# Mask rows moved in four pieces instead of eight, and three steps of an attention schedule moved, in an attention and mixture-of-experts kernel

## The chip, the cores and the metric

The kernel runs on one core of one Trainium2 chip. The metric is the device time of one execution in microseconds (us), as the median of several runs. PE is the matrix engine (TensorE) and PEld its weight loads, DVE is VectorE, ACT is ScalarE, POOL is GpSimd, and SP is the engine whose queue issues most of the DMAs.

## The reference

Three layers follow one another. The first is an attention in which a query sees only keys that fall to the same of 16 centroids:

```
q_assign = np.argmax(np.einsum('bhsd,hcd->bhsc', q_n, c_n), axis=-1)
k_assign = np.argmax(np.einsum('bhsd,hcd->bhsc', k_n, c_n), axis=-1)
mask = q_assign[:, :, :, None] == k_assign[:, :, None, :]
scores = scale * np.matmul(q, k.transpose(0, 1, 3, 2))
scores = np.where(mask, scores, -1000000000.0)
attn = softmax(scores)
return np.matmul(attn, v)
```

There are 2 batches of 8 heads, 768 positions and 64 dimensions a head. The second layer sends each of the 1536 tokens to one of 8 experts (512 to 1024 to 512), the third is a gated unit (512 to 1536 to 512). Only the first layer's code is changed.

## The kernel before, in words

The attention works on pairs of heads, eight of them (n = 0 to 7), and each pair has 12 steps: 2 heads times 6 blocks of 128 queries, so 96 steps g in all. In every step the function `run` walks through a fixed list of tokens, `CFG["order"]`, and each token issues some instructions. Since every engine works through its own instructions in order, this list sets the order on each engine. `S` is `soft(g + 1)`: ACT computes the exponential `P` of a block's scores, with the row maximum as bias. `Q` is `qk(g + 2)`: PE computes the scores `s` of a block two steps ahead (four matmuls, `Ak`/`Aq` and then `kB`/`qB`), and DVE takes their negative row maximum `nm`. `T0` and `T1` are `pt(g, 0)` and `pt(g, 1)`: PE transposes `P` in two halves of three blocks into `t`, and ACT copies the first half to `PT`, DVE the second. `E` is `evac`: in the second of every three steps it takes the output sum `acc` out of PSUM, half of it through ACT (`ol`), and DVE adds the two halves into `O`. `O` is `onat`: where `outs` has an entry, PE brings the output into natural order (`on`) and DVE computes the reciprocal sums `rs` and writes logits `lg` and outputs `x`. `V0` is `pv`: in the first of every three steps PE multiplies `PT` with v into `acc`. `B0` and `B1` issue the preparation of the next pair.

The preparation has eight parts, each at a step that `CFG["offs"]` gives relative to the first step of the pair that is running. `q0`, `q1`, `k0`, `k1` (function `tr`) transpose half of the next pair's q or k (`trp`); ACT and DVE or POOL split them into a high part `H`, a low part `L` and a sum `X`, and after the second half SP issues the moves of `H` and `L` into the tiles `A` and `B` that the scores read. `a` (`assign`) multiplies `X` with the centroids (`asp`, copied by ACT to `as`). `t` (`pick`) transposes that (`ast`), and DVE takes the maximum and marks where it is met (`mxa`, `eqa`). `f` makes the one-hot rows `oh`, and `m` (`mask`) transposes them (`otp`), ACT writes them, scaled for k to 0 and a large negative number, to `oT`, and SP moves 16 rows each into `qB` and `kB`. The scores of a block come out masked that way, by 16 more rows of the contraction.

The PSUM tile that `trp`, `asp`, `ast`, `otp` and `on` write, tag `mm` of pool `ps_m`, exists once. The scores have two buffers (`ps_s`), the transposes of `P` two (`ps_t`), `acc` one (`ps_a`). For a half of a pair whose index is not the last, `outs` puts `on` at step 0 (half 0) or 3 (half 1) of the following pair, as `CFG["oc"]` says; in the last pair other numbers hold.

Of the kernel before, what the change touches and what calls it, by code (L numbers as in the profile page):

```python
# [11 lines left out]
F32R = mybir.dt.float32r  # L12
I32 = mybir.dt.int32
U32 = mybir.dt.uint32
AF = mybir.ActivationFunctionType
# [8 lines left out]
class Attention:  # L24
# [119 lines left out]
    def tr(self, n, nm, half):  # L144
# [10 lines left out]
        nc.scalar.activation(out=Ht[:, sl], in_=flat, func=AF.Copy, scale=s)  # L155
        if CFG["xe"]["qk".index(nm)] == "a":
            nc.scalar.activation(out=X[:, sl], in_=flat, func=AF.Copy, scale=s)
# [130 lines left out]
    def mask(self, n):  # L288
        nc, st = self.nc, self.pairs[n]
        C, HJ, HS = self.C, self.J // 2, self.S // 2  # L290
        oT = self.one.tile([128, HS], F32R, tag="oT", name="oT")
        ps = self.ps_m.tile([128, HJ, 128], F32, tag="mm", name="otp")
        for jj in range(HJ):
            nc.tensor.transpose(ps[:, jj, :], st["oh"][:, jj, :], self.ident)
        nc.scalar.activation(out=oT, in_=ps.rearrange("p j t -> p (j t)"), func=AF.Identity, scale=self.sc[:, 0:1],
                             bias=self.sc[:, 1:2])
        for half in range(2):
            sl = slice(half * HS, (half + 1) * HS)
            for si, nm in enumerate("qk"):
                Bt = st["B" + nm]  # L300
                r0 = (2 * half + si) * 2 * C
                self.move(Bt[64:64 + C, 0, sl], oT[r0:r0 + C])
                self.move(Bt[64 - C:64, 1, sl], oT[r0 + C:r0 + 2 * C])

    def prep_steps(self, n):
        return dict(q0=lambda: self.tr(n, "q", 0), k0=lambda: self.tr(n, "k", 0), q1=lambda: self.tr(n, "q", 1),
# [122 lines left out]
    def run(self, cent, gate, early, fill, after):  # L429
# [6 lines left out]
        for n in range(1, self.NP):  # L436
            s0 = 2 * J * (n - 1)
            st = self.prep_steps(n)
            for nm, o in CFG["offs" if n > 1 else "offs1"]:
                if n == 1 and nm in ("q0", "q1"):  # L440
                    continue
                bg.setdefault(s0 + o, []).append(st[nm])
            if n + 1 < self.NP:
                bg.setdefault(s0 + CFG["load"], []).append(lambda n=n: self.load(n + 1, "qk"))
            if n > 1:
# [31 lines left out]
        for G in range(4 * self.NP - 1):  # L477
            n, half, r = self.group(G)
            if r == 1:
                outs[(G + 1) * HJ + CFG["oc"][half if n + 1 < self.NP else 2]] = n, half  # L480

        def trickle(g, tok):
            if chains and tok in CFG["mt" if g < NG - 2 * J else "mt2"] and g >= chains[0][0]:
                if next(chains[0][1]) is None:
                    moves.append(chains.pop(0)[1])
            if moves and tok == CFG["pt"] and g % CFG["pe"] == 0:
                if next(moves[0], 0) == 0:
                    moves.pop(0)
# [44 lines left out]
            pass  # L533


CFG = {'px': 'a', 'mt2': ['T0', 'S'], 'mt': ['B1'], 'pt': 'V0', 'pe': 1, 'ms': [5, 2, 1], 'mr': 5, 'order': ['S', 'Q', 'T0', 'T1', 'E', 'B0', 'O', 'V0', 'B1'], 'offs': [['q0', -4], ['q1', -2], ['k0', -1], ['k1', 1], ['a', 2], ['t', 3], ['f', 6], ['m', 7]], 'xe': 'da', 'me': 'a', 'ee': 'a', 'ec': 1, 'oc': [3, 3, 2], 'offs1': [['q0', 4], ['k0', 0], ['k1', 1], ['a', 2], ['t', 3], ['f', 5], ['m', 6], ['q1', 0]], 'load': 0}


class Router:
# [662 lines left out]
```

## Time and profile before

| | |
|---|---|
| median of 3 runs | 826.34 us (826.06 to 828.03) |
| the profiled execution | 829.75 us, of which the trace's span is 827.7 us |
| PE busy in the span | 785.4 us (95%) |
| DVE, ACT, POOL busy | 531.2, 380.8, 191.9 us |
| granted clock of PE, mean | 0.993 of full speed |

The profile is of one execution. The attention lasts from the start to about 300 us, the experts to about 525, the gated unit to the end. Busy time of PE is no measure of its speed, since matmuls are pipelined and their ends are modelled; where PE is held up is read from the waits and from the distances of starts.

### The profile page before, as it was taken

To read this page: it belongs to the slowest core of one execution; us is meant where nothing else is said; L and a number is where in the kernel's file an instruction comes from. 1 tells how busy PE (TensorE), PEld (TensorE's weight loads), DVE (VectorE), ACT (ScalarE), POOL (GpSimd) and SP (SyncE) were. 2 spreads that over 40 slices of the span, in tenths; PEclk is the share of its full clock that TensorE was granted. 3 is DMA by queue.
4 is the path that set the end of the run, shared out by engine and by line. 5 is a ranking of instruction groups with operands and counts; after the bars stand their busy time and mean duration, and the time that the engine had idled before them with its cause. 6 is when DMAs were issued, how large, how long until landed. Compare 5 with 4: busy or idle time off the path is not lost. (4 is left out here: it accounts for less than half of the span.)

```text
span 827.7 us, 12686 instructions
## 1 busy us (share of the span) xinstructions
PE 785.4 (95%) x4791; PEld 656.6 (79%) x4791; DVE 531.2 (64%) x871; ACT 380.8 (46%) x697; POOL 191.9 (23%) x212
## 2 busy tenths in 40 slices
PE   7998999988989998999999999999999999999996
PEld 6766666656756678999999997878888888888885
DVE  5675676766776775765665563677767676667433
ACT  5674675755666644455454452444423223222110
POOL 5110110101120145500000000244333323332335
PEclk9999999999999999999999999999999999999999
DMA  9864848527153127666665751223221212210012
GB/s 201 191 135 131 209 129 246 128 63 173 28 155 111 39 92 265 216 212 195 195 204 192 227 170 50 85 93 103 76 77 56 72 51 76 72 57 1 0 52 101
DMA packets 94209, 102.03 MB, mean 123 GB/s; under 512 B 30752, under 2 KB 78752, under 8 KB 94144
## 3 DMA queue, kind: packets, MB, share of 16 engines
q1 hardware_dynamic: 89280, 89.33, 38.2%
q0 software_dynamic: 1920, 6.29, 2.0%
q10 hardware_dynamic: 2944, 5.54, 1.9%
q8 instruction: 41, 0.67, 0.4%
q14 instruction: 24, 0.20, 0.1%
HBM read 68.21 MB, written 12.58 MB: 98 GB/s over the span
## 5 line engine op out<-in xcount | busy, mean ns | idle before, releaser
L341 DVE TENSOR_REDUCE nm<-s 128x1 f32<-128x768 f32 x96 | 91.4, 953 | 71.3 <-PE s L338 70.7
L351 ACT ACTIVATE P<-s,nm 128x768 f32<-128x768 f32 x96 | 87.0, 907 | 9.4 <-DVE nm L341 5.8
L370 ACT COPY PT<-t 128x384 f32<-128x384 f32 x96 | 46.3, 482 | 84.9 <-PE t L367 84.3
L367 PE MATMUL t<-ident,P 128*128 128x128 f32 x576 | 82.1, 277 | 0.9 <-ACT PT L370 0.5
L1027 POOL TENSOR_TENSOR W1l<-cm,W1h 128x512 fp32r<-128x512 f32 x18 | 23.4, 1303 | 235.0 <-ACT W1h L1026 235.0
L367 PEld LDWEIGHTS t<-ident,P 128*128 128x128 f32 x576 | 69.7, 143 | 7.4 <-DVE PT L372 1.2
L844 PE MATMUL hp<-Xl,W1h 128*128 128x256 f32 x256 | 73.3, 286 | 0.3 <-DVE Xl L837 0.3
L844 PE MATMUL hp<-Xh,W1h 128*128 128x256 f32 x256 | 73.3, 286 | 0.2 <-ACT Xh L836 0.2
L844 PE MATMUL hp<-Xh,W1l 128*128 128x256 f32 x256 | 73.1, 285 | 0.0
L844 PE MATMUL yp<-Hhh,W2h 128*128 128x256 f32 x256 | 73.1, 285 | 0.0
L844 PE MATMUL yp<-Hhh,W2l 128*128 128x256 f32 x256 | 72.5, 283 | 0.0
L844 PE MATMUL yp<-Hhl,W2h 128*128 128x256 f32 x256 | 72.4, 283 | 0.0
L386 PE MATMUL acc<-PT,ldv 128*64 128x384 f32 x384 | 69.7, 495 | 0.2 <-DVE rm L634 0.2
L1054 POOL TENSOR_TENSOR ghl<-u,ghh 128x512 fp32r<-128x512 f32 x36 | 49.9, 1385 | 75.0 <-ACT ghh L1053 75.0
L338 PE MATMUL s<-Ak,Aq 128*128 128x384 f32 x192 | 59.1, 389 | 6.6 <-ACT P L351 6.6
L1073 DVE TENSOR_TENSOR acc<-o,acc 128x512 f32<-128x512 f32 x60 | 41.2, 692 | 31.0 <-PE o L1065 31.0
L1051 DVE TENSOR_TENSOR u<-sg,g 128x512 f32<-128x512 f32 x36 | 24.8, 688 | 54.0 <-ACT sg L1050 54.0
L338 PE MATMUL s<-kB,qB 80*128 80x384 f32 (+1 forms) x192 | 52.1, 347 | 5.6 <-DMA kB<-oT 4.8
L338 PEld LDWEIGHTS s<-Ak,Aq 128*128 128x128 f32 x192 | 29.3, 192 | 32.8 <-ACT P L351 23.1
L1053 ACT CAST ghh<-u 128x512 fp32r<-128x512 f32 x36 | 22.4, 622 | 67.9 <-DVE u L1052 67.9
L372 DVE COPY PT<-t 128x384 f32<-128x384 f32 x96 | 52.5, 547 | 1.3 <-PE t L367 1.3
L844 PEld LDWEIGHTS hp<-Xl,W1h 128*128 128x128 f32 x256 | 49.9, 195 | 0.5 <-DVE Xl L837 0.5
(269 smaller groups left out, 1972.7 us busy)
## 6 DMA issues: line engine op xcount, KB each, us to landing
raw<-in_moe_w SPq DMA_DIRECT2D x64, 512.0 KB, 4.3
Ak<-Hk SPq DMA_DIRECT2D x32, 192.0 KB, 4.8
moe_rows<-zero SPq DMA_DIRECT2D x8, 768.0 KB, 5.6
raw<-in_moe_w_gate SPq DMA_DIRECT2D x12, 512.0 KB, 3.6
raw<-in_moe_w_val SPq DMA_DIRECT2D x12, 512.0 KB, 3.6
raw<-in_moe_w_out SPq DMA_DIRECT2D x12, 512.0 KB, 3.5
xr<-moe_rows ACTq DMA_DIRECT2D x7, 768.0 KB, 6.2
ldq<-in_q SPq DMA_DIRECT2D x16, 192.0 KB, 4.2
```

Source lines behind the costliest of these rows:

```text
L338: nc.tensor.matmul(ps[:, c, 0:HS], lhsT=ql[:, qs], rhs=kr[:, c * HS:(c + 1) * HS], start=a == 0, stop=a == 1)
L341: nc.vector.tensor_reduce(out=nm, in_=ps[:, :, 0:HS], axis=AX.XY, op=ALU.max, negate=True)
L351: nc.scalar.activation(out=P, in_=ps[:, :, 0:HS], func=AF.Exp, bias=nm, accum_out=self.pairs[n]["sum"][:, i, r:r + 1])
L367: nc.tensor.transpose(ps[:, jj, :], P[:, a, jj * 128:(jj + 1) * 128], self.ident)
L370: nc.scalar.copy(out=PT[:, js, cs], in_=ps)
L372: nc.vector.tensor_copy(PT[:, js, cs], ps)
L386: nc.tensor.matmul(acc[c * D:(c + 1) * D], lhsT=v[:, c * HJ + j], rhs=PT[:, c * HJ + j, :], start=j == 0, stop=j == HJ - 1, tile_position= ...
L844: self.nc.tensor.matmul(out, lhsT=W[a][:, k, cols], rhs=mov[b][:, k, :], start=i == 0, stop=i == n - 1)
L1027: nc.gpsimd.tensor_tensor(out=l, in0=m, in1=h.bitcast(F32), op=ALU.subtract)
L1051: nc.vector.tensor_tensor(out=u, in0=sg, in1=ps[0], op=ALU.mult)
L1054: nc.gpsimd.tensor_tensor(out=hl[:, fc], in0=u, in1=hh[:, fc].bitcast(F32), op=ALU.subtract)
L1073: nc.vector.tensor_tensor(out=a, in0=p[t], in1=a, op=ALU.add)
```

## The change

Three things are changed. The mask rows: `mask` writes the two halves of the sequence side by side into an `oT` of 64 rows and 768 columns, by two ACT instructions of 64 partitions each, and moves 16 rows of 768 columns by four DMAs, where there was one ACT instruction of 128 partitions and eight DMAs of 16 rows and 384 columns. The order of tokens: `E` stands behind `S`, in front of `Q`, and no longer behind `T1`. The steps: `q1` runs at -3 in place of -2, and the natural-order output of half 1 at 4 in place of 3.

```
     def mask(self, n):
         nc, st = self.nc, self.pairs[n]
         C, HJ, HS = self.C, self.J // 2, self.S // 2
-        oT = self.one.tile([128, HS], F32R, tag="oT", name="oT")
+        oT = self.one.tile([4 * C, 2 * HS], F32R, tag="oT", name="oT")
         ps = self.ps_m.tile([128, HJ, 128], F32, tag="mm", name="otp")
         for jj in range(HJ):
             nc.tensor.transpose(ps[:, jj, :], st["oh"][:, jj, :], self.ident)
-        nc.scalar.activation(out=oT, in_=ps.rearrange("p j t -> p (j t)"), func=AF.Identity, scale=self.sc[:, 0:1],
-                             bias=self.sc[:, 1:2])
         for half in range(2):
-            sl = slice(half * HS, (half + 1) * HS)
-            for si, nm in enumerate("qk"):
-                Bt = st["B" + nm]
-                r0 = (2 * half + si) * 2 * C
-                self.move(Bt[64:64 + C, 0, sl], oT[r0:r0 + C])
-                self.move(Bt[64 - C:64, 1, sl], oT[r0 + C:r0 + 2 * C])
+            p = slice(half * 4 * C, (half + 1) * 4 * C)
+            nc.scalar.activation(out=oT[:, half * HS:(half + 1) * HS], in_=ps[p].rearrange("p j t -> p (j t)"),
+                                 func=AF.Identity, scale=self.sc[p, 0:1], bias=self.sc[p, 1:2])
+        for si, nm in enumerate("qk"):
+            for r, p0 in ((0, 64), (1, 64 - C)):
+                c0 = (2 * si + r) * C
+                self.move(st["B" + nm][p0:p0 + C, r], oT[c0:c0 + C])
...
-CFG = {'px': 'a', 'mt2': ['T0', 'S'], 'mt': ['B1'], 'pt': 'V0', 'pe': 1, 'ms': [5, 2, 1], 'mr': 5, 'order': ['S', 'Q', 'T0', 'T1', 'E', 'B0', 'O', 'V0', 'B1'], 'offs': [['q0', -4], ['q1', -2], ['k0', -1], ['k1', 1], ['a', 2], ['t', 3], ['f', 6], ['m', 7]], 'xe': 'da', 'me': 'a', 'ee': 'a', 'ec': 1, 'oc': [3, 3, 2], 'offs1': [['q0', 4], ['k0', 0], ['k1', 1], ['a', 2], ['t', 3], ['f', 5], ['m', 6], ['q1', 0]], 'load': 0}
+CFG = {'px': 'a', 'mt2': ['T0', 'S'], 'mt': ['B1'], 'pt': 'V0', 'pe': 1, 'ms': [5, 2, 1], 'mr': 5, 'order': ['S', 'E', 'Q', 'T0', 'T1', 'B0', 'O', 'V0', 'B1'], 'offs': [['q0', -4], ['q1', -3], ['k0', -1], ['k1', 1], ['a', 2], ['t', 3], ['f', 6], ['m', 7]], 'xe': 'da', 'me': 'a', 'ee': 'a', 'ec': 1, 'oc': [3, 4, 2], 'offs1': [['q0', 4], ['k0', 0], ['k1', 1], ['a', 2], ['t', 3], ['f', 5], ['m', 6], ['q1', 0]], 'load': 0}
```

The changed file is one line shorter from `mask` on, so a line of `qk` that is L338 before is L337 after.

On PE, steps 3 and 4 of a middle pair. Before:

```order
L338 MATMUL s<-kB_93,qB_91 128x384 x2
L367 MATMUL t<-ident,P 128x128 x6
L213 MATMUL ast<-ident,as 128x128 x3
L416 MATMUL on<-R,O 128x144 x3
L386 MATMUL acc<-PT,ldv 64x384 x6
L338 MATMUL s<-Ak,Aq 128x384 x2
L338 MATMUL s<-kB_93,qB_91 128x384 x2
L367 MATMUL t<-ident,P 128x128 x6
```

And in the changed kernel, on the same engine at the same place:

```order
L337 MATMUL s<-kB_93,qB_91 128x384 x2
L366 MATMUL t<-ident,P 128x128 x6
L213 MATMUL ast<-ident,as 128x128 x3
L385 MATMUL acc<-PT,ldv 64x384 x6
L337 MATMUL s<-Ak,Aq 128x384 x2
L337 MATMUL s<-kB_93,qB_91 128x384 x2
L366 MATMUL t<-ident,P 128x128 x6
L415 MATMUL on<-R,O 128x144 x3
```

The output matmuls `on` have moved from behind `ast` to behind the next step's transposes of `P`.

On ACT, steps 7 to 10 of a middle pair. Before:

```order
L351 ACTIVATE P,sum<-s,nm 128x768
L370 COPY PT<-t 128x3x128
L397 COPY ol<-acc 64x384
L295 ACTIVATE oT<-otp,sc 128x384
L351 ACTIVATE P,sum<-s,nm 128x768
L370 COPY PT<-t 128x3x128
L155 ACTIVATE Hq<-trp 128x384
L351 ACTIVATE P,sum<-s,nm 128x768
L370 COPY PT<-t 128x3x128
L351 ACTIVATE P,sum<-s,nm 128x768
L370 COPY PT<-t 128x3x128
L397 COPY ol<-acc 64x384
```

And in the changed kernel, from the same exponential on:

```order
L350 ACTIVATE P,sum<-s,nm 128x768
L396 COPY ol<-acc 64x384
L369 COPY PT<-t 128x3x128
L297 ACTIVATE oT<-otp,sc 64x384 x2
L350 ACTIVATE P,sum<-s,nm 128x768
L369 COPY PT<-t 128x3x128
L155 ACTIVATE Hq<-trp 128x384
L350 ACTIVATE P,sum<-s,nm 128x768
L369 COPY PT<-t 128x3x128
L155 ACTIVATE Hq<-trp 128x384
L350 ACTIVATE P,sum<-s,nm 128x768
L396 COPY ol<-acc 64x384
```

The evacuation `ol` has moved in front of the copy of `PT`, `oT` is two instructions, and the second `Hq` follows the first after one exponential.

On SP's queue, from the first mask move of a middle pair to q's first moves. Before:

```order
L132 DMA qB_90<-oT 16x384 x2
L132 DMA kB_92<-oT 16x384 x2
L132 DMA qB_90<-oT 16x384 x2
L132 DMA kB_92<-oT 16x384 x2
L132 DMA Aq<-Hq 64x768
L132 DMA qB_91<-Hq 64x768
```

And in the changed kernel, on the same queue:

```order
L132 DMA qB_90<-oT 16x768 x2
L132 DMA kB_92<-oT 16x768 x2
L132 DMA Aq<-Hq 64x768
L132 DMA qB_91<-Hq 64x768
L132 DMA Aq<-Lq 64x768
```

The first mask move into `kB` is the third in the queue; before, the first one for half 1 was the seventh.

## Rows read from the trace of the kernel before

**Rows 1.** Waits of PE, 36 to 322 us: engine, line, releaser: us, times, longest.

```profile
PE on L416 <- DVE rs L411: 10.1, 6, 1.7
PE s L338 <- ACT P L351: 4.9, 14, 0.9
PE s L338 <- DMA kB<-oT: 4.8, 6, 1.8
...
PE trp L151 <- DVE Lq L160: 1.7, 5, 0.3
```

**Rows 2.** Waits of the weight loads in the same stretch.

```profile
PEld on L416 <- issue: 11.3, 6, 1.9
...
PEld asp L203 <- issue: 1.2, 6, 0.2
```

**Rows 3.** Timeline of PE, 93 to 146: start, us, operation, count, [idle before, releaser].

```profile
98.05 0.97 PE L416 MATMUL on<-R,O 128*128 128x144 f32 x6 [1.68 <-DVE rs L411]
...
101.85 0.82 PE L367 MATMUL t<-ident,P 128*128 128x128 f32 x6
102.42 0.59 PE L338 MATMUL s<-Ak,Aq 128*128 128x384 f32 x2
...
103.21 0.94 PE L367 MATMUL t<-ident,P 128*128 128x128 f32 x6
104.43 0.61 PE L338 MATMUL s<-Ak,Aq 128*128 128x384 f32 x2 [0.28 <-ACT P L351]
...
109.54 0.49 PE L294 MATMUL otp<-ident,oh 128*128 128x128 f32 x3
...
116.81 0.44 PE L338 MATMUL s<-kB,qB 80*128 80x384 f32 x1 [0.35 <-DMA kB<-oT]
...
119.95 0.55 PE L151 MATMUL trp<-ident,ldk 128*128 128x128 f32 x3 [0.34 <-DVE Lq L160]
```

**Rows 4.** Timeline of DVE in the same stretch.

```profile
102.12 0.96 DVE L341 TENSOR_REDUCE nm<-s 128x1 f32<-128x768 f32 x1 [2.39 <-PE s L338]
...
122.57 0.17 DVE L411 TENSOR_SCALAR rs<-sum 128x6 f32<-128x6 f32 x1
...
123.19 0.55 DVE L420 TENSOR_TENSOR x<-on,rs 128x384 f32<-128x384 f32 x1
```

**Rows 5.** Groups of instructions, 40 to 430 us: count, busy us, mean ns, idle before.

```profile
L370 ACT COPY PT<-t 128x384 f32<-128x384 f32 x89 | 42.9, 482 | 81.7 <-PE t L367 81.0
...
L399 DVE TENSOR_TENSOR O<-acc,ol 64x384 f32<-64x384 f32 x31 | 16.9, 546 | 0.6
...
L397 ACT COPY ol<-acc 64x384 f32<-64x384 f32 x31 | 14.8, 476 | 2.7 <-PE acc L386 1.9
```

**Rows 6.** Timeline of ACT, 93 to 146 us.

```profile
102.88 0.48 ACT L397 COPY ol<-acc 64x384 f32<-64x384 f32 x1
103.38 0.90 ACT L351 ACTIVATE P<-s,nm 128x768 f32<-128x768 f32 x1
...
110.42 0.67 ACT L295 ACTIVATE oT<-otp,sc 128x384 fp32r<-128x384 f32 x1
110.99 0.89 ACT L351 ACTIVATE P<-s,nm 128x768 f32<-128x768 f32 x1
```

**Rows 7.** SP's timeline, then the list of DMAs: count, KB each, us to landing.

```profile
114.92 1.22 SPq L132 DMA_DIRECT2D kB<-oT  x2
...
kB<-oT SPq DMA_DIRECT2D x28, 24.0 KB, 1.9
...
qB<-oT SPq DMA_DIRECT2D x1, 48.0 KB, 2.9
kB<-oT SPq DMA_DIRECT2D x1, 48.0 KB, 2.5
```

**Rows 8.** Stages: us, busy (count) of PE, PEld, DVE, ACT, POOL, PEclk, DMA, GB/s.

```profile
189.00:191.20 2.20, 2.20 (x12) 2.10 (x11) 1.97 (x5) 1.36 (x3) 1.00 (x1) 0.50 0.46 102
...
358.00:411.00 53.00, 52.70 (x440) 52.35 (x440) 33.01 (x35) 27.05 (x35) 0.00 (x0) 1.00 0.66 208
```

## The prediction

> **What bounds the kernel now.** I read four views: the waits of TensorE (PE), its timeline through one pair of heads, ACT and DVE beside it, and the stages. In the expert part PE is busy 52.70 of 53 us while the DMA engines move at 0.66 [rows 8], so nothing but less PE work helps there; the change doesn't touch it. In the attention PE stands still some five us in every pair, and the waits view says for what: the output matmul `on` behind DVE's `rs` (10.1 us, six times), scores behind ACT's exponential (4.9), scores behind the mask moves (4.8, six times, longest 1.8), transposes of k behind `Lq` (1.7, five times) [rows 1]. The reader should see that three of these four come in the same number as the middle pairs: they are stalls of the schedule's pattern, not accidents. They also cost more than they show: PE's ends are modelled, so an idle of 0.28 before the scores at 104.43 goes with a start-to-start distance of 1.22 us after the transposes at 103.21, where the same six transposes at 101.85 give way after 0.57 [rows 3]. 0.65 was lost, 0.28 is shown. I add 0.25 to an idle, less than that difference, where no such pair of rows stands. PE's weight loads say the same of `on`: 11.3 us over six, 1.9 each, against 1.68 of idle [rows 2, 3].
>
> I count the twelve steps of a pair from 0; qk runs two steps ahead, so step 10 issues the next pair's first scores.
>
> **`on`, one step later (half 1: `oc` 3 to 4).** At step 3 `pick` puts its transposes `ast` into the only buffer of `ps_m`, and `on` wants the same buffer at once. It waits until DVE has taken the maximum and `eqa` out: 1.9 us. At step 4 the buffer has long been read, since the 2 us of `acc` and a whole step lie between. The 1.9 goes, six times. The 0.65 lost at 104.43 goes too: between the scores of steps 4 and 6 PE now has `on` as well (0.97 us busy [rows 3]), and that is longer than the wait for P. What is late next: DVE's four instructions of the outputs take 1.17 us from the first to the last when nothing holds them (122.57 to 123.74) [rows 4] and fall into two short steps without `acc`, so the second half of step 6's transposes waits for step 5's PT copy on DVE. That costs between 0 and 1.17; by DVE's sequence from 102.12 on (maximum, copy, these four, maximum, copy: about 5.1 us after the scores start, where PE wants its buffer at 4.7) I take 0.35. Moving `on` between transposes and scores loses some 0.2 in changes of kind (estimate from the distances above). Per pair 1.9 + 0.65 - 0.35 - 0.2 = 2.0; **six pairs, 12.0 us**.
>
> **Mask moves, four for eight.** The moves run in one queue, SP, 1.22 us for two; in the old order the one that the first scores need is the seventh, issued at 114.92, and PE goes on at 116.81, 1.89 later [rows 3, 7]. Now it is the third, so 1.25 after the first, with 48 KB in place of 24. The median landing of 24 KB is 1.9; the two 48 KB moves of the first pair took 2.9 and 2.5 [rows 7]. The price: ACT now evacuates 64 partitions twice, and a copy of 64 partitions (476 ns) is no cheaper than one of 128 (482) [rows 5]. One oT blocks ACT 0.57 us, from 110.42 to the P at 110.99 [rows 6]. otp ends at 110.03 [rows 3], so two of them put that P at about 111.25, 0.25 later, and PE waits for this P (one of the 14 waits in [rows 1]): 0.25 is on the path. The second oT ends near 111.35, the third move starts at 112.6 and lands by 115.1 to 115.5; PE asked at 116.81 - 0.35 = 116.46, so it no longer waits: 0.35 + 0.25 = 0.6 gone.
> The Trainium skill, page "DMA: Bandwidth & Descriptors", section "Anatomy of one DMA", gives a DMA a fixed cost of about 2.0 us that doesn't grow with size; by it (an estimate) the 48 KB would land in about 2.1. The 24 KB rows agree and the 48 KB rows don't (2.5 and 2.9), perhaps for what else was then in flight. By the rule the sum is the same, since nobody waits either way; the second rival below would have 0.04 in place of 0.08.
>
> **q1 one step earlier (-2 to -3).** Its three transposes are moved, not added. k's transposes at step 11 waited 0.34 for `Lq` of q1 [rows 1, 3], 0.6 with the hidden part; now two steps lie between. q1 itself follows q0 by one step, as k0 followed q1, but no O stands before `Lq` there any more, and the longer wait for P gives it time: taken as 0. Its six DMAs leave one step sooner behind only four mask moves on SP; they wait for q's own halves there, so no load is held up. Without O's distance, step 11's second transposes may wait for a PT copy: 0 to 0.55 (one O, 546 ns [rows 5]), I take 0.3. With the masks: 0.6 + 0.6 - 0.25 - 0.3 = 0.65; **five pairs, 3.2 us**.
>
> **The late ones.** Of the six waits for moves four are near 0.35, so 4.8 - 6 x 0.35 = 2.7 lies in two late landings. Behind one of them the granted clock is 0.50 for 2.2 us [rows 8], the lower of the two levels: 1.1 us of work. With a margin of 1 us or more most of both should be gone: **3.8 us**, but irregular; an execution without late landings has none of it to give.
>
> **O ahead of the scores (`E` moved).** On ACT `ol` goes ahead of the PT copy, into idle time: 81.7 us stand before 89 such copies [rows 5]. On DVE O goes ahead of the row maximum. `ol` starts when `acc` is done, that is when the next scores start; 0.48 + 0.55 later plus two handovers O is done about 1.2 after it, and the maximum was ready at 1.08: up to 0.15 late, 31 times (loss at most 4.6). Against it P no longer stands behind `ol`: the maximum from 102.12 ended at 103.08 and P began at 103.38 [rows 4, 6], 0.2 to be had. Taken as 0 where P bounds. Where the second half of k feeds `asp`, ACT is 0.5 earlier: of the 1.2 us there [rows 2] I take **0.9**. If the cover is gone, this is the third rival. The last pair's mask gain and the tail (at the end `ol` delays a PT copy that PE waits for, about 0.5) cancel.
>
> **Sum.** 12.0 + 3.2 + 3.8 + 0.9 = 19.9, from the profiled execution's 829.75: 809.9. That execution stands 3.4 above the median of 826.34, about the 3.8 of the late landings. If the others had none, the gain is 16.1 and the median 810.2. I predict **810 us**.
>
> **Rivals.**
> First, the `on` stall moves: DVE's 1.17 us falls wholly on PE's path in the short steps, as waits of `t` for PT and of scores for P. For it: 1.17 is more than the 0.65 that `on` covers. Against: `acc` follows in step 6 and gives DVE time to catch up. Six times 0.8 more: 815.
> Second, the masks are no sooner: the second oT and slower 48 KB landings eat what four issues save. 6 x 0.6 = 3.6: 814, with late landings 817.
> Third, slower: the evacuation comes into the path. DVE is in order, so O ahead of the maximum makes maximum, P and the scores two steps on wait for `ol`. If ACT is late with the P before it, each of 31 evacuations costs `ol` + O whole, 1.02 us [rows 5]: 31.6, so 842. It decides at 16.1 / 31 = 0.52 each. Against: ACT's idle above.
> Fourth, the attention ends sooner and nothing follows, if weight loads set the expert part: 826. Against: [rows 8].
>
> **Numbers.** Forecast 0.70, own range 804 to 814 (loss of the O order 4.6 up; the 0.35, 0.3 and 0.2 not coming and late landings gone everywhere, some 6 down). First rival 0.11, second 0.08, third 0.05, fourth 0.03; 0.03 for a larger gain. The range 803 to 818 takes in the first two. Under 0.3% (2.5 us) a measurement of this kernel tells nothing. Faster 0.92, same 0.03, slower 0.05.
>
> **What would show it.** `on` behind `rs` gone from PE's waits; scores behind kB's moves and `trp` behind `Lq` gone; scores behind P fewer at step 6, a little longer behind the two oT; new small waits of `t` for PT on DVE; some 2.6 us less from one pair's `on` to the next's. Wrong would be: waits of scores for P at every third step (third rival), or `t` for PT above 1 us a pair (first).

## The result, and the profile after

The changed kernel takes 807.83 us as a median of 4 runs (806.93 to 809.11), beside 827.18 (826.06 to 829.65) for the kernel before: ratio 0.9763, 95% interval 0.9734 to 0.9793. So it is 19 us faster; 810 us was predicted, from a median before of 826.34. The profiled execution took 806.93, with a span of 805.2 against 827.7. Lines from `mask` on stand one lower (L338 is now L337).

Waits of PE after, over the attention (engine, line, releaser: us, times, longest), from 36 to 305 us, to be set against [rows 1]:

```profile
PE s L337 <- ACT P L350: 3.4, 6, 1.1
PE t L366 <- DVE PT L371: 2.7, 8, 0.6
```

`on` behind `rs` (10.1), scores behind the moves (4.8) and `trp` behind `Lq` (1.7) are all gone. What came new is `t` behind PT on DVE (one wait of 0.5 before). Scores behind P became fewer, 6 for 14, but longer each: 3.4 us in total for 4.9. The timeline of PE through the pair that stands in [rows 3] shows where they are (start, us, operation, count, idle before and releaser):

```profile
93.72 0.90 PE L415 MATMUL on<-R,O 128*128 128x144 f32 x6
...
95.16 0.82 PE L366 MATMUL t<-ident,P 128*128 128x128 f32 x6
95.73 0.59 PE L337 MATMUL s<-Ak,Aq 128*128 128x384 f32 x2
...
96.51 0.49 PE L366 MATMUL t<-ident,P 128*128 128x128 f32 x3
97.28 0.55 PE L366 MATMUL t<-ident,P 128*128 128x128 f32 x3 [0.28 <-DVE PT L371]
...
101.31 0.49 PE L294 MATMUL otp<-ident,oh 128*128 128x128 f32 x3
...
104.25 0.62 PE L337 MATMUL s<-Ak,Aq 128*128 128x384 f32 x2 [0.47 <-ACT P L350]
...
108.68 0.51 PE L337 MATMUL s<-kB,qB 80*128 80x384 f32 x2
...
111.34 0.49 PE L151 MATMUL trp<-ident,ldk 128*128 128x128 f32 x3
...
125.43 0.90 PE L415 MATMUL on<-R,O 128*128 128x144 f32 x6
```

From `on` to `on` it is now 31.71 us; 2.6 us less than before was predicted, and 2.6 is what went. `on` at 93.72, the scores at 108.68 and `trp` at 111.34 follow without idle. The scores at 104.25 now wait, and ACT shows for what:

```profile
100.02 0.48 ACT L396 COPY ol<-acc 64x384 f32<-64x384 f32 x1 [0.84 <-PE acc L385]
...
101.83 1.35 ACT L297 ACTIVATE oT<-otp,sc 64x384 fp32r<-64x384 f32 x2 [0.18 <-PE otp L294]
103.21 0.90 ACT L350 ACTIVATE P<-s,nm 128x768 f32<-128x768 f32 x1
```

`ol` is out of the way early, but two `oT` of 1.35 together stand in front of P. It starts 1.90 after `otp`; before it was 1.45 (109.54 to 110.99, [rows 3, 6]).

The list of DMAs after (count, KB each, us to landing):

```profile
qB<-oT SPq DMA_DIRECT2D x15, 48.0 KB, 2.1
kB<-oT SPq DMA_DIRECT2D x15, 48.0 KB, 2.1
```

So 48 KB land in 2.1 us, against 1.9 for 24 KB [rows 7]: twice the bytes cost 0.2. The prediction gave 2.1 as the estimate by the Trainium skill (page "DMA: Bandwidth & Descriptors", section "Anatomy of one DMA"), and held the 2.9 and 2.5 of one pair against it; 15 landings of each kind decide for the estimate. (The section is written for GpSimd's path; these moves are in SP's queue. And a step of 0.2 from 24 to 48 KB is not what a cost that doesn't grow with size would give.)

### The profile page after: what moved, and what is told of

Its sections match the earlier page's. It is cut to its first block, busy times and chain, and to the rows that moved or that the text cites. A ratio compares the mean times of both kernels' runs of the same rounds, so it can differ in the third digit from the quotient of the medians.

```text
span 805.2 us, 12688 instructions
## 1 busy us (share of the span) xinstructions
PE 777.8 (97%) x4791; PEld 652.3 (81%) x4791; DVE 530.3 (66%) x871; ACT 387.9 (48%) x704; POOL 191.8 (24%) x212
## 5 line engine op out<-in xcount | busy, mean ns | idle before, releaser
L337 PE MATMUL s<-Ak,Aq 128*128 128x384 f32 x192 | 58.3, 384 | 5.1 <-ACT P L350 4.8
L1052 ACT CAST ghh<-u 128x512 fp32r<-128x512 f32 x36 | 22.4, 621 | 67.5 <-DVE u L1051 67.5
L337 PEld LDWEIGHTS s<-Ak,Aq 128*128 128x128 f32 x192 | 28.9, 189 | 29.3 <-ACT P L350 19.1
L337 PE MATMUL s<-kB,qB 80*128 80x384 f32 (+1 forms) x192 | 49.8, 340 | 0.8 <-ACT kB L276 0.7
```

Of the source, the lines that this page charges most:

```text
L337: nc.tensor.matmul(ps[:, c, 0:HS], lhsT=ql[:, qs], rhs=kr[:, c * HS:(c + 1) * HS], start=a == 0, stop=a == 1)
```

## A measure for the experiments

Single executions differ by 2 us before the first `otp` (last section), so beside the ratio I give what the trace shows of each kernel between its seven `otp`: the shortest distance from one to the next, which is a pair without accidents (before, 34.30), and the **excess**, how much the five distances from the second `otp` to the seventh exceed five such pairs (the first has one step more). The starts of `otp` before are 73.75, 109.54, 143.84, 178.17, 215.12 and 250.12: 176.37 - 5 x 34.30 = 4.87 of excess. In the table, **P** is the time from `otp` to the start of the P that follows `oT` on ACT, at the third `otp`. Each ratio is against the kernel before, measured beside it.

Executions differ in another thing too, the granted clock that is recorded with each. The 23 of the kernel before beside the first four experiments go from 823.86 us at a mean clock of 0.999 to 830.07 at 0.990. A straight line through all 125 executions with a recorded clock (my estimate: 0.62 us per 0.001, with a scatter of 0.5 us left) sets every kernel to one clock; the column **at 0.994** is the time there, good to about 0.3 us. It assumes that a kernel has no part in which clock its executions get, and no run tests that. But the three groups of the kernel before, with medians of 827.36, 828.56 and 829.72, come together to within 0.3 us by it. Where ratio and column say different things, the ratio also holds the clocks that the two kernels happened to get.

| kernel | ratio (95%) | at 0.994, us | shortest pair | excess | P |
|---|---|---|---|---|---|
| before | 1 | 827.8 | 34.30 | 4.87 | 1.45 |
| after | 0.9763 (0.9734 to 0.9793) | 808.8 | 31.72 | 0.76 | 1.90 |
| before, `on` alone | 0.9877 (0.9849 to 0.9905) | 817.0 | 32.62 | 2.43 | 1.45 |
| before, masks alone | 0.9999 (0.9980 to 1.0018) | 827.3 | 34.51 | 1.12 | 2.26 |
| before, q1 alone | 0.9964 (0.9948 to 0.9981) | 825.4 | 33.82 | 2.62 | 1.45 |
| before, `E` alone | 0.9893 (0.9861 to 0.9925) | 818.8 | 33.17 | 2.83 | 1.10 |
| before, `ol` early alone | 0.9934 (0.9907 to 0.9960) | 824.2 | 33.73 | 2.39 | 1.10 |
| before, `on` and `E` | 0.9746 (0.9724 to 0.9769) | 806.8 | 31.25 | 2.98 | 1.11 |
| after without `on` | 0.9879 (0.9860 to 0.9898) | 818.9 | 33.63 | 0.57 | 1.90 |
| after without masks | 0.9701 (0.9682 to 0.9720) | 805.6 | 30.96 | 2.74 | 1.10 |
| after without q1 | 0.9740 (0.9718 to 0.9762) | 806.9 | 31.50 | 0.94 | 1.91 |
| after without `E` | 0.9837 (0.9820 to 0.9853) | 815.9 | 32.63 | 0.80 | 2.25 |
| after, half of `oT` on DVE | 0.9696 (0.9674 to 0.9719) | 806.3 | 31.38 | 0.90 | 1.10 |
| after, three `oT` | 0.9806 (0.9781 to 0.9831) | 813.3 | 32.36 | 0.79 | 2.61 |

## The experiments

**The four edits one by one, on the kernel before.** The theory is the prediction's own sum, and its rivals with it. Of the line `CFG` only the changed entry is shown. First `on`:

```
-'oc': [3, 3, 2]
+'oc': [3, 4, 2]
```

> The kernel before with one number changed: the natural-order output of half 1 runs at step 4 in place of 3. Theory (each stall is a term of its own, and on's term is 12.0 us): on no longer waits behind rs and the scores of step 6 no longer wait for P, but in the old order O stands on DVE between the PT copy and rs of step 4, so step 6's second transposes wait up to 0.47 us longer than with the whole change: a gain of 9 to 12 us. First rival (the stall only moves): a gain of 7 us or less, with the difference in waits of t for PT. A third reading, that the output step pays only together with the earlier evacuation: under 5 us.

816.71 us against 827.36, 10.6 less by the medians; 1.7 in an undisturbed pair. PE's waits:

```profile
PE t L367 <- DVE PT L372: 4.9, 8, 0.8
...
PE s L338 <- ACT P L351: 2.7, 8, 0.6
```

`on` behind `rs` is gone, and DVE's four output instructions come back as `t` behind PT. That wait is bigger here, 4.9 us, than in the changed kernel, 2.7, because O still stands at its old place on DVE (4.9 as well in the changed kernel without `E`, 2.5 in the kernel before with `on` and `E`). The term was right in mechanism and nearly in size.

Then the masks (the `mask` function of the changed kernel in the kernel before):

```
-        oT = self.one.tile([128, HS], F32R, tag="oT", name="oT")
+        oT = self.one.tile([4 * C, 2 * HS], F32R, tag="oT", name="oT")
...
+                self.move(st["B" + nm][p0:p0 + C, r], oT[c0:c0 + C])
```

> The kernel before with the new mask function alone (two ACT instructions, four moves). Theory: the six waits of scores for kB's moves go (6 x 0.6), the exponential behind the second oT comes 0.25 us later in seven pairs (1.8), late landings give 0 to 3.8: a gain of 2 to 5.5 us, and no wait of scores for DMA. Second rival (48 KB moves land too late, or the second oT eats the gain): same or slower, with waits for DMA left.

827.46 against 827.36: nothing. Yet the trace is not unchanged. Its waits, and ACT behind one `otp` (which starts at 110.47):

```profile
PE on L415 <- DVE rs L410: 10.1, 6, 1.7
PE s L337 <- ACT P L350: 6.9, 15, 1.4
PE trp L151 <- ACT oT L297: 2.1, 5, 0.4
```

```profile
110.85 0.48 ACT L396 COPY ol<-acc 64x384 f32<-64x384 f32 x1
111.35 1.35 ACT L297 ACTIVATE oT<-otp,sc 64x384 fp32r<-64x384 f32 x2
112.73 0.90 ACT L350 ACTIVATE P<-s,nm 128x768 f32<-128x768 f32 x1
```

The waits for moves are gone, all six, the late ones too, which is the theory's part. In their place PE waits for P (6.9 for 4.9) and, to get the buffer that `oT` still reads, before `trp` (2.1, new). P starts 2.26 after `otp` for 1.45. What the moves gave, ACT took: the second rival's mechanism and its size, though not its "slower 48 KB landings".

q1:

```
-['q1', -2]
+['q1', -3]
```

> The kernel before with q1 at -3 in place of -2 alone. Theory: k's transposes of step 11 no longer wait for Lq (5 x 0.6), and PE comes about 0.3 us later to the mask moves in step 10, so that their wait shrinks by as much: a gain of 2 to 4 us. Rival: q1 itself waits for Lq of q0, one step behind it as k0 was behind q1: no gain, a wait of trp of ldq for Lq in five pairs.

824.77, 2.6 less; `trp` behind `Lq` is gone, and the moves' waits fell too, as the theory had it; they fell further, from 4.8 us in six to 1.9 in three. The rival's wait of q's transposes for `Lq` isn't there:

```profile
...
PE s L338 <- ACT P L351: 5.2, 15, 0.9
PE s L338 <- DMA kB<-oT: 1.9, 3, 0.8
```

The order of tokens:

```
-'order': ['S', 'Q', 'T0', 'T1', 'E', 'B0', 'O', 'V0', 'B1']
+'order': ['S', 'E', 'Q', 'T0', 'T1', 'B0', 'O', 'V0', 'B1']
```

> The kernel before with the evacuation in front of the scores alone. Theory: about nothing, 0 to 2 us gained (ol in ACT's idle, the exponential 0.1 to 0.2 earlier at the steps where it bounds, asp 0.15 earlier). Third rival of the prediction (the evacuation comes into the path through DVE's order): slower by 5 us or more, with scores waiting for P at every third step.

817.94 against 827.36: 9.4 less, ten times what was predicted, and the third rival has no sign for it. ACT and then PE in this kernel:

```profile
105.47 0.48 ACT L397 COPY ol<-acc 64x384 f32<-64x384 f32 x1 [0.76 <-PE acc L386]
...
107.30 0.67 ACT L295 ACTIVATE oT<-otp,sc 128x384 fp32r<-128x384 f32 x1 [0.18 <-PE otp L294]
107.87 0.89 ACT L351 ACTIVATE P<-s,nm 128x768 f32<-128x768 f32 x1
```

```profile
106.77 0.49 PE L294 MATMUL otp<-ident,oh 128*128 128x128 f32 x3
...
108.91 0.62 PE L338 MATMUL s<-Ak,Aq 128*128 128x384 f32 x2
...
115.67 0.82 PE L367 MATMUL t<-ident,P 128*128 128x128 f32 x6
116.32 0.52 PE L151 MATMUL trp<-ident,ldk 128*128 128x128 f32 x3
```

`oT` waits for `otp` alone, P starts 0.35 sooner, and the scores at 108.91 have no wait. Before, the same scores had one:

```profile
112.02 0.62 PE L338 MATMUL s<-Ak,Aq 128*128 128x384 f32 x2 [0.30 <-ACT P L351]
```

`trp` of k at 116.32 follows its transposes without one as well, with q1 still at -2: O no longer stands between PT and `Lq` on DVE. DVE ahead of that `trp`, before and then here:

```profile
118.17 0.55 DVE L372 COPY PT<-t 128x384 f32<-128x384 f32 x1
118.75 0.55 DVE L399 TENSOR_TENSOR O<-acc,ol 64x384 f32<-64x384 f32 x1
119.33 0.56 DVE L160 SCALAR_TENSOR_TENSOR Lq<-trp,Hq 128x384 fp32r<-128x384 f32 x1
```

```profile
115.06 0.55 DVE L372 COPY PT<-t 128x384 f32<-128x384 f32 x1
115.69 0.56 DVE L160 SCALAR_TENSOR_TENSOR Lq<-trp,Hq 128x384 fp32r<-128x384 f32 x1
```

With PE's starts of the two shortest pairs laid side by side from `otp` on, the 1.13 falls into four places: 0.35 at the scores behind `oT` and P, 0.5 at k's transposes, 0.1 at `asp`, and 0.15 at the scores of step 6, which waited for P at 104.43 [rows 3].

**Which half of `E` does it.** `evac` cut in two: ACT's copy at the early place, DVE's add at the old one.

```
-'order': ['S', 'Q', 'T0', 'T1', 'E', 'B0', 'O', 'V0', 'B1']
+'order': ['S', 'E0', 'Q', 'T0', 'T1', 'E', 'B0', 'O', 'V0', 'B1']
...
+                elif tok == "E0" and c == CFG["ec"] and G >= 0:
+                    self.evac0(G)
...
```

> The kernel before, with only ACT's copy ol moved to the early place, and the add O on DVE left behind the second half of the transposes. Theory (ACT's part and DVE's part both count): scores wait less for P as in the kernel with the whole evacuation moved, about 0.34 + 0.16 + 0.15 a pair, 4 to 5 us, so 822 to 823, while trp goes on waiting for Lq as before. Rival (ACT's copy alone does all of it): 817 to 819, and the wait for Lq gone. Second rival (O ahead of Lq and of the row maximum is what counts): 826 to 828.

823.16 against 829.72, ratio 0.9934, which is 5.5 us; at one clock it is 3.6 of the 9.0 that `E` alone gives. Both halves count. PE's waits:

```profile
...
PE s L338 <- DMA kB<-oT: 3.9, 6, 1.3
PE trp L151 <- DVE Lq L160: 2.1, 6, 0.3
...
PE s L338 <- ACT P L351: 0.6, 2, 0.3
```

ACT's half takes scores behind P from 4.9 to 0.6; `Lq` stays at 2.1. By undisturbed pairs ACT's half is 0.57 of the 1.13, DVE's the rest.

**Each edit taken out of the changed kernel.** The same four lines, the other way round.

> The changed kernel with the natural-order output of half 1 back at step 3, the three other edits kept. Theory (terms add): 8 us faster than before, about 12 slower than the changed kernel, on waiting behind rs 1.7 us six times again. If the parts need one another, the loss against the changed kernel is more than 12.

819.04 against 828.56; the 10.1 us behind `rs` are back, 1.91 in a pair. That is 11.5 in six pairs and 10.1 at one clock, where about 12 was expected. Alone `on` gave 10.8 at one clock, so it gains as much without the other edits as with them.

> The changed kernel with the evacuation back behind T1. Theory: the evacuation is worth little alone, but in the changed kernel O behind the PT copy makes rs to x, the next maximum and the next PT copy 0.47 us later in step 4, six times: 2 to 4 us slower than the changed kernel, waits of t for PT about 0.5 longer each. Rival: no difference.

815.32 against 828.56, some 6 to 7.5 us worse than the changed kernel; 0.91 in a pair. The loss is over the 2 to 4 expected, as the gain of `E` alone was.

> The changed kernel with q1 back at -2. Theory: k's transposes wait for Lq again, 0.34 shown and 0.6 lost, in five pairs, against 0.3 of waits of t for PT that q1's old place would hide: 1.5 to 3 us slower than the changed kernel. Rival: no difference, since O no longer stands before Lq on DVE in the new order, and that, not q1's step, took the wait away.

806.3 against 828.56: q1 is worth nothing here, and rather costs, 0.22 in a pair (31.50 for 31.72) and 2.0 us at one clock. With `E` early `trp` behind `Lq` doesn't come back at -2, and with four moves there is no wait for moves to be covered.

> The changed kernel with the old mask function (one ACT instruction, eight moves). Theory: 2 to 5.5 us slower than the changed kernel, scores waiting for kB's moves again, and longer than before (0.35), since PE now comes to them earlier in its pair by what the other edits took away (about 0.3 less wait for P, 0.3 later through q1): 0.3 to 0.7 us, late ones apart. Rival: no difference, the saved P time balances the DMA wait.

803.9 against 828.56. The interval (0.9682 to 0.9720) lies below that of the changed kernel, so **the masks cost time in it**: 0.76 in a pair, some of it given back by the excess, 2.74 for 0.76.

**Is it the second `oT`?** Two doses. One more `oT` on ACT (it writes the second half twice, the same values), or one less (DVE writes the second half).

```
-        for half in range(2):
+        for half in (0, 1, 1):
```

> The changed kernel, with ACT writing the second half of oT twice over (the same values), so three oT instructions. Theory (ACT in front of P is the path there): 0.6 to 0.7 us more in each of seven pairs, 4.2 to 4.9, so 811 to 813. Rival (the loss of the four moves lies in their landing or in SP's queue, not in ACT): the scores' wait for P grows a little, and the time stays within 807 to 809.

813.78 against 829.72, ratio 0.9806. ACT:

```profile
105.60 2.05 ACT L297 ACTIVATE oT<-otp,sc 64x384 fp32r<-64x384 f32 x3 [0.18 <-PE otp L294]
107.68 0.90 ACT L350 ACTIVATE P<-s,nm 128x768 f32<-128x768 f32 x1
```

P starts 0.71 later and an undisturbed pair is 0.64 longer (32.36 for 31.72), so 0.64 of the third copy's 0.7 is on the path. In seven pairs that is 4.5 us; at one clock it is 4.4 (by the ratios 3.6). The time is above the 811 to 813 expected, but so is the kernel before, measured beside it, by 2.4. No wait for DMA comes back, so the rival is out. ACT's `oT` holds PE up in two ways, though: P stands behind it, and `trp` needs the buffer that `oT` reads (3.9 us in five waits here; the changed kernel's waits show none).

```
...
+                nc.vector.tensor_scalar(out=o, in0=i, scalar1=self.sc[p, 0:1], scalar2=self.sc[p, 1:2], op0=ALU.mult,
+                                        op1=ALU.add)
```

> The changed kernel, but the second half of oT is written by DVE, beside ACT's first half. Theory (the second oT on ACT holds up P of step 9, and that is what the four moves cost): the wait of the scores for P behind oT goes, the first scores of step 9 to those of step 11 take 3.6 to 3.8 in place of 4.4 us, seven times 0.6 to 0.8, so 803 to 804.5. Rival (DVE has no room there: its half delays the row maximum of step 10, or takes as long as the ACT one): 806 to 809, with the wait for P moved on by one step.

804.72 against 829.72, ratio 0.9696: faster than the changed kernel, no different from the one with the old masks. DVE in it, then PE:

```profile
104.57 0.69 DVE L301 TENSOR_SCALAR oT<-otp,sc 64x384 fp32r<-64x384 f32 x1
105.28 0.96 DVE L344 TENSOR_REDUCE nm<-s 128x1 f32<-128x768 f32 x1
```

```profile
105.31 0.55 PE L151 MATMUL trp<-ident,ldq 128*128 128x128 f32 x3 [0.17 <-DVE oT L301]
105.61 0.60 PE L341 MATMUL s<-Ak,Aq 128*128 128x384 f32 x2
```

The wait for P is gone (P 1.10 after `otp`), but the row maximum now starts behind DVE's `oT` and `trp` waits 0.17 for it, so of 0.76 a pair 0.34 comes back, and the excess stays as low as with four moves (0.90). Both theory and rival had a part of it.

**`on` and `E` without the other two.**

> The kernel before with on at step 4 and the evacuation in front of the scores, with the eight old moves and q1 at -2. Theory (these two make the whole gain, q1 gives nothing once the evacuation is early): 803 to 805, as the changed kernel with the old moves did. Rival (q1 helps when PE isn't slowed by the second oT, since q's moves then leave earlier): 805.5 to 808.

808.65 against 829.72, ratio 0.9746, not to be told from the changed kernel by its interval. So masks and q1 together give nothing; by the pair (31.25 for 31.72) and at one clock (806.8 for 808.8) they cost. Against the kernel with q1 as well (0.9701) it is slower, which was the rival's side, but not for the rival's reason. PE in this kernel, then in the one with q1 at -3, both with the old moves:

```profile
110.02 0.34 PE L338 MATMUL s<-kB,qB 80*128 80x384 f32 x1
110.71 0.44 PE L338 MATMUL s<-kB,qB 80*128 80x384 f32 x1 [0.36 <-DMA kB<-oT]
...
111.65 0.49 PE L151 MATMUL trp<-ident,ldq 128*128 128x128 f32 x3
```

```profile
107.51 0.49 PE L151 MATMUL trp<-ident,ldq 128*128 128x128 f32 x3
...
110.47 0.80 PE L338 MATMUL s<-kB,qB 80*128 80x384 f32 x2
```

At -3 the transposes of q stand ahead of the scores that need the moves, at -2 behind them. They fill the time in which the move lands. This is also why q1 alone cut the waits for moves, as was expected of it.

## Why the prediction came out right

The time, the range and the pair's 2.6 us came true. Several steps did not; their errors cancelled, so that the total came out so close is in part luck. From median to median 16 us were forecast (826.34 to 810), and 19 came. Between the first and the seventh `otp` before and after differ by 19.3 us: six pairs of 34.30 - 31.72 = 2.58, which is 15.5, and 3.8 more: 4.1 of excess, less 0.3 in the first distance. Of the last `on`'s 22.4 (295.67 to 273.31) another 1.2 lie behind the seventh `otp`, and 1.9 ahead of the first, where executions differ anyway.

- **`on`, 2.0 a pair.** Right: 1.7 alone, 1.9 inside the changed kernel. The 0.35 for `t` behind PT was somewhat low: its two halves at 96.51 and 97.28 after stand 0.77 apart, where six transposes without a wait give way after 0.57 (95.16 to 95.73), three of them after 0.29; so about 0.5.
- **O ahead of the scores, "taken as 0 where P bounds", 0.9 in all.** This step failed: 1.13 a pair alone, 0.91 in the changed kernel, so 5.5 to 6.8 in six. The 0.9 was for `asp`, and most of that came, 0.1 a pair. What failed is the 0 beside it. The step looked at one P only, that of 103.38, where it saw 0.2 to be had against O's delay of the row maximum; 0.15 came there. At the P of 110.99 `ol` stood ahead of `oT` and so of P, worth 0.35. And O ahead of `Lq` on DVE was worth 0.5; the prediction names it, but books that wait for q1. The `ol` stood in ACT's timeline of the kernel before, right ahead of the `oT` of [rows 6]:

```profile
109.91 0.48 ACT L397 COPY ol<-acc 64x384 f32<-64x384 f32 x1
```

- **Masks and q1, 0.65 a pair.** Failed in sign: pairs with `on` and `E` alone take 31.25, with these two as well 31.72, so they cost 0.47. Two of the four terms came: laid side by side from `otp` on, these pairs show 0.6 back where the wait for the moves was, and 0.3 lost at k's transposes, which wait for `t` behind PT. The 0.25 for the second `oT` was too small: P moved by 0.45 against before, but before had `ol` in that queue; with `ol` gone the right comparison is 1.10 against 1.90, and 0.8 is the price. And the 0.6 for `Lq` was credited to q1, though `E` had already taken that wait away.
- **Late landings, 3.8.** Right in mechanism: over all fourteen kernels the excess is 2.4 to 4.9 with the eight moves (seven kernels) and 0.6 to 1.1 with four (seven). They are not irregular, though, as the prediction has it: in every trace with the eight moves the waits near 80 and near 180 us are the late ones, 0.7 to 1.8 us each. Only the profiled execution of before had 4.9; the mean of the other six is 2.7, so 1.8 to 1.9 is the usual worth, and the 3.8 belongs to that one execution. That late landings are what sets executions of the kernel before apart is not shown either; their times follow the granted clock with a scatter of 0.5 us.
- **The "some five us in every pair"** of standstill is what a stretch of 53 us shows; between the `otp` at 109.54 and the next PE was idle for 2.96. The sum doesn't use it.
- **Rivals.** The first (DVE's outputs on the path) came in small, as the 0.5 at 97.28. The second named what happened to the masks; it didn't show in the total, since `E` brought as much more as the masks brought less: 1.1 a pair down, 0.9 up. The third, slower by O ahead of the maximum, is ruled out by the kernel with `E` alone, the fourth by the time itself.

Alone the four edits give 1.7 - 0.2 + 0.5 + 1.1 = 3.1 a pair, together 2.6. They don't add, since `E` and q1 both answer to the wait for `Lq`, masks and q1 both to the moves, and `E` frees the ACT time that the second `oT` then takes (masks cost 0.2 alone, 0.76 with the rest).

The fastest kernels measured are the changed one with the old masks (0.9701) and the one with half of `oT` on DVE (0.9696). Which of the two is better stays open (805.6 and 806.3 at one clock). The ratios put 5 to 5.5 us between these and the changed kernel, their traces from the first `otp` to the last `on` 2.2 to 2.6; at one clock it is 3.2 and 2.5, so most of what the ratios have beyond the traces is the clock that the executions got.

## What to carry to other kernels

When several edits are made at once, price each against a kernel that has the others already: a wait that one edit removes can't be sold twice, and a queue that one edit empties changes what the next one costs. On an engine that works in order, list what stands ahead of the instruction that others wait for at every place where the moved one occurs, not only where the trace was read first. Where a DMA's wait is short, work that is needed anyway and can be put ahead of it does part of what a faster DMA would: q's transposes at -3 covered 0.3 of the 0.6 a pair.

## What the runs showed of the hardware

Splitting one ACT instruction by partitions doubles its time: `oT` takes 0.67 us with 128 partitions [rows 6], and also with 64 at the same 384 columns, in a row of the kernel with half of it on DVE:

```profile
103.68 0.67 ACT L299 ACTIVATE oT<-otp,sc 64x384 fp32r<-64x384 f32 x1 [0.18 <-PE otp L294]
```

The clock at the start isn't the same in every execution. Window 20 to 24 us, before and then after (us, busy (count) of PE, PEld, DVE, ACT, POOL, PEclk, DMA, GB/s):

```profile
20.00:24.00 4.00, 4.00 (x17) 3.89 (x18) 1.51 (x2) 2.19 (x6) 0.01 (x1) 0.57 0.84 222
```

```profile
20.00:24.00 4.00, 3.85 (x29) 3.54 (x28) 2.85 (x4) 3.31 (x9) 1.00 (x1) 1.00 0.97 222
```

Before, PE was at the lower of its two levels (1.2 of 2.4 GHz) for most of it, after it was at the upper one. The kernel with `on` alone also had 1.00 there; the other twelve, before among them, had 0.50 to 0.63. It follows no edit that I can see: before and after, PE had the same 1.37 us of idle just ahead of it, waiting for P (to 19.91 and to 19.67). The first `otp` stood between 34.7 and 38.8 us. The change isn't credited with it.
